# An attention and FFN kernel: the first 16 score tiles transposed by TensorE, the weights' low halves made by GpSimd, the weight conversions later in the order

## The chip, the cores and the metric

The kernel runs on one core of a Trainium2 chip. The metric is the device time of one execution in microseconds (us), taken as the median of several runs. The engines of the core are TensorE (PE in the profile, with its weight loads as PEld), VectorE (DVE), ScalarE (ACT), GpSimd (POOL) and SyncE (SP), whose queue issues all DMAs here.

## The reference

Attention with a threshold, followed by a feed-forward network (FFN) over the same tokens:

```python
# q, k, v: (8 batches, 8 heads, 576 tokens, 64), float32
scores = scale * q @ k^T
thresh = max(scores, axis=-1) - tau
scores = where(scores >= thresh, scores, -1e9)
attn   = exp(scores - max) / (sum(exp(scores - max)) + 1e-9)
x      = (attn @ v) as (4608 tokens, 512)        # heads side by side
# w_in: (512, 2048), w_out: (2048, 512): they arrive as float64
h      = relu(x @ w_in)
out    = (s * h * h + b) @ w_out                 # (4608, 512) float32
```

## The kernel before, in words

**Order.** Every piece of work is handed to a planner (`Plan`) with an engine, a cost in ns, the keys that it reads and writes, and a due number `at`. The planner runs the pieces through its own model: whenever an engine is free, it takes from those that are ready the one with the lowest due number. The result is a fixed order for each engine; on the chip each engine goes through its list in that order. Due numbers count tiles: tile i is the i-th score tile.

**Attention.** A visit is one batch, one pair of heads and one half (256) of the first 512 queries. It has four tiles, each 128 queries of one head by all 576 keys; half of the visits have a fifth tile for the last 64 queries of both heads. There are 64 visits and 288 tiles. For a tile:

- PE makes the scores (L211; the fifth tile L202), into PSUM banks `s0` and `s1`.
- DVE scales them, takes the row minimum of the negated scores and copies to `sm` (L221).
- ACT adds tau to that minimum (L225, one column) and takes the exponential into `em` (L227).
- DVE masks and sums (L230), then takes the reciprocal (L233).
- POOL multiplies the rows by it (L234), in place in `em`. `sm` and `em` have two buffers each.
- DVE transposes `em` in 32 x 32 blocks into `tr` (L238 and, for the last 64 keys, L240).
- Four DMAs on SP's queue (L244) bring the blocks of `tr` to their partitions in `er`.

When a visit's tiles are in `er`, PE multiplies with V (PV, L255) into bank `pv`, and ACT copies the result to `x` (L259, tails L262).

**Loads.** A visit's loads (L180 to L192: K, Q, two of V and, for the last 64 keys of V, two more) are due six tiles ahead. K's columns are permuted on the host, before the launch.

**Weights.** The FFN is cut into 16 chunks of 128 hidden units. Chunk f has a load of w_in and one of w_out (L280, L283, 512 KB each, due at 2 + f). It is then converted from float64 to a high and a low half in the fp32r type, twice each step (for w_in and w_out): ACT L315, DVE L318, DVE L320, ACT L324 (the high half), DVE L326 (the low half: value minus high half). This conversion is due at `WEIGHTS_AT + WEIGHTS_EACH * f`, that is 6 + 1.2f.

**FFN.** A block is 256 tokens. Its x is split into a high and a low half (ACT L368, DVE L370: `stage`). Each of 16 steps multiplies x by one chunk of w_in (L385, bank `h`), ACT applies relu, square and the high half (L388, L390, L391), POOL makes the low half gl (L392), and PE multiplies by the chunk of w_out (L398, bank `o`). There are 18 blocks, 288 steps. Block 0 follows visit 3: its stage is due at 17.5, step f at 17.5 + 1.2f, and so it needs one new chunk at each step. Block 1 follows visit 7. During block 0, four sums over w_out's columns are also made on PE (L337).

**Filling.** Before and between the first tiles, PE runs matmuls without use (L468, `keep_busy`): 16 at the start and 5 after each of the first five tiles.

Of the kernel before, what the change touches and what calls it, by code (L numbers as in the profile page):

```python
# [14 lines left out]
LOAD_AHEAD = 6  # L15
SCORES_AHEAD, VALUES_AFTER = 1, 2
FFN_AFTER = 2.5
BUSY, BUSY_TILES, BUSY_EACH = 16, 5, 5
WEIGHTS_AT, WEIGHTS_EACH = 6, 1.2
FIRST_WEIGHTS = 4  # L20


# [77 lines left out]
def tile_attention_ffn(ctx: ExitStack, tc: tile.TileContext, qT, kT, v, tau, w_in, w_out, s, b, out):  # L100
    nc = tc.nc
    P = 128
# [23 lines left out]
    def const(name, shape, dt=F32):  # L126
        return cp.tile(shape, dt, name=name)
# [41 lines left out]
    class Visit:
        def __init__(self, n, bi, pair, u, tail):  # L170
            self.n, self.bi, self.pair, self.u, self.tail, self.end = n % 2, bi, pair, u, tail, False
            self.h2 = slice(2 * pair, 2 * pair + 2)
            self.kq = [("k", self.n), ("q", self.n)]
            self.kd = [("qd", self.n, j) for j in range(2)]
            self.kv = [("v", self.n, x) for x in range(4)]
            self.nb = (NB + (T if tail else 0)) // 32

        def load(self, at):
            n, bi, h2 = self.n, self.bi, self.h2
            dma(295, lambda: nc.sync.dma_start(out=kb[n], in_=kT[bi, h2].rearrange("h d s -> (h d) s")), [], [("k", n)], at)  # L180
            dma(131, lambda: nc.sync.dma_start(out=qb[n], in_=qT[bi, h2, :, self.u * NB:(self.u + 1) * NB].rearrange(
                "h d s -> (h d) s")), [], [("q", n)], at)
            if self.tail:
                for j in range(2):
                    dma(16, lambda j=j: nc.sync.dma_start(out=qd[n][j * D:(j + 1) * D, j * T:(j + 1) * T],
                                                          in_=qT[bi, 2 * self.pair + j, :, M:S]), [], [self.kd[j]], at)
            for j in range(2):
                dma(131, lambda j=j: nc.sync.dma_start(
                    out=vb[n][:, j, 0:NQ], in_=v[bi, 2 * self.pair + j, 0:M, :].rearrange("(c p) d -> p c d", p=P)),
                    [], [self.kv[j]], at + 1)  # L190
            for m in range(2):
                dma(16, lambda m=m: nc.sync.dma_start(  # L192
                    out=vb[n][:, :, NQ].rearrange("(k m) h d -> k m h d", m=4)[:, m],
                    in_=v[bi, h2, M + 32 * m:M + 32 * m + 32, :].rearrange("h k d -> k h d")), [], [self.kv[2 + m]], at + 1)
# [20 lines left out]
    def tile_of(vs, i, j, t):  # L215
        ps, ks_, st8 = bank[f"s{j}"], f"st{i % 6}", st[i % 6]
        sm_k, em_k, tr_k = f"sm{i % 2}", f"em{i % 2}", f"tr{i % 2}"
        sb_, eb, to = sm[i % 2], em[i % 2], tr[i % 2]
        ev = eb[:, 0:S]

        dve((745, 830), lambda: nc.vector.tensor_scalar(  # L221
            out=sb_[:, 0:S].rearrange("p (a b) -> p a b", a=2), in0=ps[:, :, 0:HS],
            scalar1=nsc, scalar2=None, op0=ALU.mult, op1=ALU.min, accum_out=st8[:, 0:1]),
            [f"s{j}", "nsc"], [sm_k, (ks_, 0)], i - 0.6)
        act((287, 370), lambda: nc.scalar.activation(out=st8[:, 1:2], in_=st8[:, 0:1], func=AF.Identity, bias=tau0),  # L225
            [(ks_, 0), "nsc"], [(ks_, 1)], i - 0.4)
# [3 lines left out]
        dve2((940, 1010), lambda: nc.vector.scalar_tensor_tensor(  # L230
            out=eb, in0=sb_, scalar=st8[:, 1:2], in1=eb, op0=ALU.is_le, op1=ALU.mult,
            accum_out=st8[:, 2:3]), [sm_k, em_k, (ks_, 1)], [em_k, (ks_, 2)], i)
        dve((110, 165), lambda: nc.vector.reciprocal(out=st8[:, 4:5], in_=st8[:, 2:3]), [(ks_, 2)], [(ks_, 4)], i)  # L233
        pool((900, 940), lambda: nc.gpsimd.tensor_scalar(  # L234
            out=ev, in0=ev, scalar1=st8[:, 4:5], scalar2=zero, op0=ALU.mult, op1=ALU.add), [em_k, (ks_, 4)], [em_k], i)

        def blocks():
            nc.vector.transpose(out=to[:, :, 0:NQ].rearrange("p m c q -> p m (c q)"),  # L238
                                in_=ev[:, 0:M].rearrange("p (m r) -> p m r", m=4))
            nc.vector.transpose(out=to[:, 0:2, NQ], in_=ev[:, M:S].rearrange("p (m q) -> p m q", m=2))  # L240
        dve((915, 980), blocks, [em_k], [tr_k], i + 0.5)
        for n in range(4):
            jj, e = (n // 2, NB // 32 + n % 2) if t is None else (j, 4 * t + n)
            plan.add("SP", (450, 2600), lambda n=n, jj=jj, e=e: nc.sync.dma_start(  # L244
                out=er[:, vs.n, jj, e], in_=to[32 * n:32 * n + 32].rearrange("p m c q -> p m (c q)")),
                [tr_k], [("er", vs.n, jj, e)], i + 0.5)

    def with_v(vs, at):
        n, nb = vs.n, vs.nb
        ps = bank["pv"]  # L250

        def products():
            for c in range(5):
                for j in range(2):
                    nc.tensor.matmul(ps[j * D:(j + 1) * D, 0:32 * nb], vb[n][:, j, c], er[:, n, j, 0:nb, 32 * c:32 * c + 32],  # L255
                                     start=(c == 0), stop=(c == 4))
        pe(10.5 * 0.85 * 32 * nb, products, vs.kv + [("er", n, j, e) for j in range(2) for e in range(nb)], ["pv"], at)
        xk = xs[vs.bi, vs.u]
        act((340, 420), lambda: nc.scalar.copy(out=xb[xk][:, vs.pair], in_=ps[:, 0:NB]), ["pv"], [("x", xk, vs.pair)], at)  # L259
        if vs.tail:  # L260
            q = vs.bi % 4
            act((220, 300), lambda: nc.scalar.copy(out=xt[:, vs.pair, q * T:(q + 1) * T], in_=ps[:, NB:NB + T]), ["pv"],  # L262
                [("xt", q, vs.pair)], at)
# [22 lines left out]
    def weights(f, at):  # L286
# [11 lines left out]
        def tmp():  # L298
            if ("tmp", f) not in lazy:
                lazy["tmp", f] = sb(tag, [P, 2, DM], F32)  # L300
            return lazy["tmp", f]
# [10 lines left out]
            return tmp().bitcast(I32)[:, u]  # L312
        for u, k in (0, "i"), (1, "o"):
            kr, kt = (f"w{f}", k), (tag, u)
            act((570, 670), lambda u=u: nc.scalar.activation(  # L315
                out=tmp()[:, u], in_=words(1, u).bitcast(F32), func=AF.Prelu, scale=2.0 ** -112, alpha=-2.0 ** 32),
                [kr], [kt] if u else [tag, kt, (tag, 1)], at)
            dve2((410, 480), lambda u=u: nc.vector.tensor_scalar(  # L318
                out=y(u), in0=y(u), scalar1=3, scalar2=None, op0=ALU.logical_shift_left), [kt], [kt], at)
            dve2((610, 690), lambda u=u: nc.vector.scalar_tensor_tensor(  # L320
                out=y(u), in0=words(0, u), scalar=29, in1=y(u), op0=ALU.logical_shift_right, op1=ALU.bitwise_or),
                [kr, kt], [kt], at)
        for u, k in (0, "i"), (1, "o"):
            act((520, 620), lambda u=u: nc.scalar.copy(out=w()[:, u, 0], in_=tmp()[:, u]), [(tag, u)],  # L324
                wkeys(f) if not u else [(f"w{f}", "o")], at)
            dve2((620, 700), lambda u=u: nc.vector.tensor_tensor(out=w()[:, u, 1], in0=tmp()[:, u],  # L326
                                                                 in1=w()[:, u, 0].bitcast(F32), op=ALU.subtract),
                 [(tag, u), (f"w{f}", k)], [(f"w{f}", k)], at)


# [235 lines left out]
```

## Time and profile before

| what | value |
|---|---|
| median of 3 runs | 1329.89 us (1328.1 to 1330.42) |
| the profiled execution, its time | 1331.58 us |
| its span in the trace | 1329.8 us |
| PE busy | 1250.4 us (94%) |
| VectorE, ScalarE, GpSimd busy | 832.7, 680.9, 503.0 us |
| mean granted TensorE clock | 0.968 |

How to read the lines: in the slices, each digit is the busy share of a fortieth of the span in tenths. In the windows, a row has the stretch and its length, the busy time (and number of instructions) of PE, PEld, DVE, ACT and POOL, the granted TensorE clock, the mean busy share of the 16 DMA engines and the GB/s that they moved. A timeline row has the start in us, the duration in us, the engine, the line, the operation, what it writes and reads, shapes and the count; a count over 1 means several merged into one row; in brackets the idle time before it and what ended it. Durations of neighbours on one engine can overlap a little, since an instruction begins before the one ahead of it has drained. A group row of the page has line, engine, operation, output and input, shapes and count, then the busy time in us and the mean ns of one, then idle time before. A row by line or tile has the count, the shortest, median and longest duration in ns, and the first and last start in us.

### The profile page before, as it was taken

How to read it: one execution, taken by the hardware profiler on the slowest of the kernel's cores; microseconds unless marked ns; L12 is line 12 of the kernel's file. 1: busy time of each engine (PE TensorE's matmuls, PEld its weight loads, DVE VectorE, ACT ScalarE, POOL GpSimd, SP SyncE). 2: the span in 40 equal slices, each digit the busy share in tenths (PEclk: the TensorE clock that was granted, in tenths of full speed). 3: DMA queues.
4: the chain of work that ended last, by engine and by line, in shares of the span. 5: the costliest groups of instructions: out<-in, count | busy, mean ns of one | idle time of the engine just before them, and what ended most of it. 6: DMA issues, size and time to landing. Idle time of an engine off the chain costs nothing.

```text
span 1329.8 us, 24065 instructions
## 1 busy us (share of the span) xinstructions
PE 1250.4 (94%) x7689; PEld 970.6 (73%) x7689; DVE 832.7 (63%) x2205; ACT 680.9 (51%) x1639; POOL 503.0 (38%) x577
## 2 busy tenths in 40 slices
PE   6448999999999999999999999999999999999997
PEld 4226766777777777777778777787777777777886
DVE  7998675767666675756666565756666575763011
ACT  4655554555445554555455544545555455554343
POOL 2212333434344444443434344434444344443210
PEclk7559999999999999999999999999999999999999
DMA  7885455555455455544454544544455444542000
GB/s 207 265 271 149 121 132 127 130 134 129 130 137 148 126 128 139 140 122 112 134 131 120 126 122 112 153 117 121 123 140 127 118 117 120 137 119 61 17 17 16
DMA packets 283822, 169.41 MB, mean 127 GB/s; under 512 B 105008, under 2 KB 268848, under 8 KB 283696
## 3 DMA queue, kind: packets, MB, share of 16 engines
q1 hardware_dynamic: 283696, 167.88, 47.9%
q8 instruction: 61, 1.00, 0.3%
q14 instruction: 65, 0.53, 0.1%
HBM read 63.96 MB, written 9.44 MB: 55 GB/s over the span
## 4 chain that ended last, share of the span: by engine, by line
PE 78%; DVE 7%; DMA 6%; SPq 4%; issue 2%; ACT 2%; POOL 0%; DVEq 0%; ACTq 0%; POOLq 0%
PE o L398 28%; PE h L385 27%; PE pv L255 12%; PE s L211 9%; DMA er<-tr 5%; SPq L244 3%; PE s L202 2%; DVE sm L221 1%; DVE em L230 1%; DVE tr L238 1%; ACT em L227 1%; DMA w<-in_moe_w_in_dram 1%; DVE w L326 1%; DMA out_dram<-oo 1%; SPq L192 0%
## 5 line engine op out<-in xcount | busy, mean ns | idle before, releaser
L385 PE MATMUL h<-xh,w 128*128 128x256 f32 x2304 | 475.3, 289 | 11.0 <-ACT g L388 10.0
L234 POOL TENSOR_SCALAR em<-em,st,zero 128x576 f32<-128x576 f32 x288 | 283.6, 986 | 459.0 <-DVE st L233 308.6
L385 PEld LDWEIGHTS h<-xh,w 128*128 128x128 f32 x2304 | 377.6, 191 | 55.8 <-ACT g L390 20.0
L398 PE MATMUL o<-w,gh 128*128 128x512 f32 x1152 | 371.1, 403 | 4.4 <-DVE oo L409 4.0
L392 POOL TENSOR_TENSOR gl<-g,gh 128x256 fp32r<-128x256 f32 x272 | 220.6, 812 | 313.1 <-issue 141.8
L227 ACT ACTIVATE em<-sm,st 128x576 f32<-128x576 f32 x288 | 222.7, 773 | 203.6 <-DVE sm L221 128.6
L385 PE MATMUL h<-xl,w 128*128 128x256 f32 x1152 | 326.1, 283 | 0.3 <-DVE xl L370 0.3
L221 DVE TENSOR_SCALAR_CACHE_REDUCE sm<-s,nsc 128x576 f32<-128x576 f32 x288 | 227.5, 809 | 123.2 <-PE s L211 83.2
L238 DVE STREAM_TRANSPOSE tr<-em 128x512 f32<-128x512 f32 x288 | 204.1, 709 | 156.6 <-DMA er<-tr 93.6
L230 DVE SCALAR_TENSOR_TENSOR em<-sm,st,em 128x577 f32<-128x577 f32 x288 | 248.0, 862 | 85.9 <-ACT st L225 53.9
L398 PEld LDWEIGHTS o<-w,gh 128*128 128x128 f32 x1152 | 199.5, 189 | 68.8 <-issue 21.0
L388 ACT ACTIVATE g<-h 128x256 f32<-128x256 f32 x288 | 109.7, 381 | 269.6 <-PE h L385 264.2
L398 PE MATMUL o<-w,gl 128*128 128x512 f32 x576 | 225.3, 391 | 1.3 <-POOL gl L392 1.3
L385 PEld LDWEIGHTS h<-xl,w 128*128 128x128 f32 x1152 | 219.9, 191 | 8.5 <-DVE xl L370 0.5
L211 PE MATMUL s<-k,q 64*128 64x288 f32 x1024 | 175.5, 446 | 33.3 <-DVE sm L221 24.3
L255 PE MATMUL pv<-er,v 128*64 128x256 f32 (+1 forms) x1280 | 188.0, 424 | 14.7 <-DMA er<-tr 12.4
L255 PEld LDWEIGHTS pv<-er,v 128*64 128x64 f32 x1280 | 99.0, 141 | 93.4 <-issue 41.2
L211 PEld LDWEIGHTS s<-k,q 64*128 64x128 f32 x1024 | 96.3, 193 | 81.2 <-DVE sm L221 32.2
L398 PEld LDWEIGHTS o<-w,gl 128*128 128x128 f32 x576 | 108.2, 188 | 28.4 <-POOL gl L392 3.1
L391 ACT CAST gh<-g 128x256 fp32r<-128x256 f32 x288 | 115.9, 402 | 15.1 <-PE o L398 8.9
L390 ACT ACTIVATE g<-g 128x256 f32<-128x256 f32 x288 | 119.2, 414 | 6.6
L225 ACT ACTIVATE st<-st,tau 128x1 f32<-128x1 f32 x288 | 81.5, 286 | 41.1 <-DVE sm L221 41.0
(46 smaller groups left out, 452.1 us busy)
## 6 DMA issues: line engine op xcount, KB each, us to landing
er<-tr SPq DMA_DIRECT2D x1152, 80.0 KB, 2.2
k<-in_k_dram SPq DMA_DIRECT2D x64, 288.0 KB, 3.1
v<-in_v_dram SPq DMA_DIRECT2D x128, 128.0 KB, 2.5
q<-in_q_dram SPq DMA_DIRECT2D x64, 128.0 KB, 2.4
w<-in_moe_w_in_dram SPq DMA_DIRECT2D x16, 512.0 KB, 4.9
w<-in_moe_w_out_dram SPq DMA_DIRECT2D x16, 512.0 KB, 4.7
out_dram<-oo SPq DMA_DIRECT2D x32, 256.0 KB, 2.3
v<-in_v_dram SPq DMA_DIRECT2D x128, 16.0 KB, 2.2
```

Of the source, the lines that this page charges most:

```text
L211: nc.tensor.matmul(bank[f"s{j}"][:, hf, 0:HS], qb[n][r, t * P:(t + 1) * P], kb[n][r, cs], start=True, stop=True)
L221: dve((745, 830), lambda: nc.vector.tensor_scalar(out=sb_[:, 0:S].rearrange("p (a b) -> p a b", a=2), in0=ps[:, :, 0:HS], scalar1=nsc, sca ...
L227: act((780, 870), lambda: nc.scalar.activation(out=ev, in_=sb_[:, 0:S], func=AF.Exp, bias=st8[:, 0:1], scale=-1.0), [sm_k, (ks_, 0)], [em_ ...
L230: dve2((940, 1010), lambda: nc.vector.scalar_tensor_tensor(out=eb, in0=sb_, scalar=st8[:, 1:2], in1=eb, op0=ALU.is_le, op1=ALU.mult, accum ...
L234: pool((900, 940), lambda: nc.gpsimd.tensor_scalar(out=ev, in0=ev, scalar1=st8[:, 4:5], scalar2=zero, op0=ALU.mult, op1=ALU.add), [em_k, ( ...
L238: nc.vector.transpose(out=to[:, :, 0:NQ].rearrange("p m c q -> p m (c q)"), in_=ev[:, 0:M].rearrange("p (m r) -> p m r", m=4))
L255: nc.tensor.matmul(ps[j * D:(j + 1) * D, 0:32 * nb], vb[n][:, j, c], er[:, n, j, 0:nb, 32 * c:32 * c + 32], start=(c == 0), stop=(c == 4))
L385: nc.tensor.matmul(ps, w[:, c, :], x[:, c, :], start=(i == 0), stop=(i == 3 * NC - 1))
L390: act((290, 390), lambda: nc.scalar.activation(out=g, in_=g, func=AF.Square), [f"g{k}"], [f"g{k}"], at)
L391: act((310, 405), lambda: nc.scalar.copy(out=hi, in_=g), [f"g{k}"], [f"gh{k}"], at)
L392: do((715, 750), lambda: eng.tensor_tensor(out=lo, in0=g, in1=hi.bitcast(F32), op=ALU.subtract), [f"g{k}", f"gh{k}"], [f"gl{k}"], at)
L398: nc.tensor.matmul(bank["o"][:, t, :], a[:, ts_], w, start=(f == 0 and i == 0), stop=(f == NF - 1 and i == 2))
```

## The change

Four things, all of which concern the opening of the kernel:

1. For the 16 tiles of the first four visits (`PE_VISITS = 4`), DVE's transposes and the four DMAs per tile go. PE transposes `em` instead, 128 columns at a time and the last 64 keys apart (five transposes a tile, into the halves of bank `o` and into bank `h`), with an identity that lies in the unused third x buffer. ACT copies the results to `er` (two copies a tile). V is loaded in another order of rows for these visits, with one DMA for the last 64 keys instead of two. The threshold addition of these tiles goes from ACT to DVE.
2. The low halves of all weight chunks are made by GpSimd instead of VectorE (L326 before).
3. `WEIGHTS_AT` goes from 6 to 12, and the planner's costs for the conversion's pieces go up.
4. 24 filling matmuls at the start, and none between the tiles; two memsets of V's last rows on GpSimd before visits 4 and 5.

```diff
-BUSY, BUSY_TILES, BUSY_EACH = 16, 5, 5
-WEIGHTS_AT, WEIGHTS_EACH = 6, 1.2
+BUSY, BUSY_TILES, BUSY_EACH = 24, 0, 5
+PE_VISITS = 4
+WEIGHTS_AT, WEIGHTS_EACH = 12, 1.2
...
+    ident = xb[2][:, 0, 0:P]
...
+            self.pe = n < PE_VISITS
...
+                rows = "(p c) d -> p c d" if self.pe else "(c p) d -> p c d"
+                dma(131, lambda j=j, rows=rows: nc.sync.dma_start(
+                    out=vb[n][:, j, 0:NQ], in_=v[bi, 2 * self.pair + j, 0:M, :].rearrange(rows, p=P)),
                     [], [self.kv[j]], at + 1)
+            if self.pe:
+                dma(32, lambda: nc.sync.dma_start(out=vb[n][0:T, :, NQ], in_=v[bi, h2, M:S, :].rearrange("h k d -> k h d")),
+                    [], self.kv[2:], at + 1)
+                return
...
+        if vs.pe:
+            dve((140, 210), lambda: nc.vector.tensor_scalar(
+                out=st8[:, 1:2], in0=st8[:, 0:1], scalar1=tau0, scalar2=None, op0=ALU.add), [(ks_, 0), "nsc"], [(ks_, 1)], i - 0.4)
+        else:
+            act((287, 370), lambda: nc.scalar.activation(out=st8[:, 1:2], in_=st8[:, 0:1], func=AF.Identity, bias=tau0),
+                [(ks_, 0), "nsc"], [(ks_, 1)], i - 0.4)
...
+        if vs.pe:
+            tp, tt = bank["o"][:, i % 2].rearrange("p (c q) -> p c q", c=NQ), bank["h"][0:T, 0:P]
+
+            def transposes():
+                nc.tensor.transpose(out=tt, in_=ev[:, M:S], identity=ident)
+                for c in range(NQ):
+                    nc.tensor.transpose(out=tp[:, c], in_=ev[:, c * P:(c + 1) * P], identity=ident)
+            pe(600, transposes, [em_k, "ident"], ["h", ("o", i % 2)], i + 0.5)
+            e = er[:, vs.n, j, 4 * t:4 * t + 4].rearrange("p n (c q) -> p c n q", c=5)
+            ke = [("er", vs.n, j, 4 * t + n) for n in range(4)]
+            act((220, 300), lambda: nc.scalar.copy(out=e[0:T, NQ], in_=tt.rearrange("p (n q) -> p n q", n=4)), ["h"], ke, i + 0.5)
+            act((640, 730), lambda: nc.scalar.copy(out=e[:, 0:NQ], in_=tp.rearrange("p c (n q) -> p c n q", n=4)),
+                [("o", i % 2)] + ke, ke, i + 0.5)
+            return
...
-            act((570, 670), lambda u=u: nc.scalar.activation(
+            act((665, 750), lambda u=u: nc.scalar.activation(
...
-            dve2((410, 480), lambda u=u: nc.vector.tensor_scalar(
+            dve2((480, 550), lambda u=u: nc.vector.tensor_scalar(
...
-            dve2((610, 690), lambda u=u: nc.vector.scalar_tensor_tensor(
+            dve2((700, 780), lambda u=u: nc.vector.scalar_tensor_tensor(
...
-            act((520, 620), lambda u=u: nc.scalar.copy(out=w()[:, u, 0], in_=tmp()[:, u]), [(tag, u)],
+            act((615, 700), lambda u=u: nc.scalar.copy(out=w()[:, u, 0], in_=tmp()[:, u]), [(tag, u)],
...
-            dve2((620, 700), lambda u=u: nc.vector.tensor_tensor(out=w()[:, u, 1], in0=tmp()[:, u],
-                                                                 in1=w()[:, u, 0].bitcast(F32), op=ALU.subtract),
+            pool((1400, 1440), lambda u=u: nc.gpsimd.tensor_tensor(out=w()[:, u, 1], in0=tmp()[:, u],
+                                                                   in1=w()[:, u, 0].bitcast(F32), op=ALU.subtract),
...
+    pool((500, 600), lambda: make_identity(nc, ident), [], ["ident"], -9.5)
...
+    for n in range(2):
+        events.append((visits[PE_VISITS - 1].last + 0.15, lambda n=n: pool(
+            (200, 240), lambda: nc.gpsimd.memset(vb[n][:, :, NQ], 0.0), [], [("v", n, 2), ("v", n, 3)],
+            visits[PE_VISITS + n].first - 5)))
```

More of the change, by code (lines that the diff above doesn't have):

```diff
@@ L7 @@
 from concourse._compat import with_exitstack
+from concourse.masks import make_identity
 F32 = mybir.dt.float32
@@ L187, in load @@
             for j in range(2):
-                dma(131, lambda j=j: nc.sync.dma_start(
-                    out=vb[n][:, j, 0:NQ], in_=v[bi, 2 * self.pair + j, 0:M, :].rearrange("(c p) d -> p c d", p=P)),
+                rows = "(p c) d -> p c d" if self.pe else "(c p) d -> p c d"
+                dma(131, lambda j=j, rows=rows: nc.sync.dma_start(
+                    out=vb[n][:, j, 0:NQ], in_=v[bi, 2 * self.pair + j, 0:M, :].rearrange(rows, p=P)),
                     [], [self.kv[j]], at + 1)
+            if self.pe:
+                dma(32, lambda: nc.sync.dma_start(out=vb[n][0:T, :, NQ], in_=v[bi, h2, M:S, :].rearrange("h k d -> k h d")),
+                    [], self.kv[2:], at + 1)
+                return
             for m in range(2):
@@ L224, in tile_of @@
             [f"s{j}", "nsc"], [sm_k, (ks_, 0)], i - 0.6)
-        act((287, 370), lambda: nc.scalar.activation(out=st8[:, 1:2], in_=st8[:, 0:1], func=AF.Identity, bias=tau0),
-            [(ks_, 0), "nsc"], [(ks_, 1)], i - 0.4)
+        if vs.pe:
[4 more added lines that the diff above has]
+                [(ks_, 0), "nsc"], [(ks_, 1)], i - 0.4)
         act((780, 870), lambda: nc.scalar.activation(
@@ L253, in products @@
             for c in range(5):
+                r = slice(0, T if vs.pe and c == NQ else P)
                 for j in range(2):
-                    nc.tensor.matmul(ps[j * D:(j + 1) * D, 0:32 * nb], vb[n][:, j, c], er[:, n, j, 0:nb, 32 * c:32 * c + 32],
+                    nc.tensor.matmul(ps[j * D:(j + 1) * D, 0:32 * nb], vb[n][r, j, c], er[r, n, j, 0:nb, 32 * c:32 * c + 32],
                                      start=(c == 0), stop=(c == 4))
@@ L258, in with_v @@
         xk = xs[vs.bi, vs.u]
-        act((340, 420), lambda: nc.scalar.copy(out=xb[xk][:, vs.pair], in_=ps[:, 0:NB]), ["pv"], [("x", xk, vs.pair)], at)
+        act((340, 420), lambda: nc.scalar.copy(out=xb[xk][:, vs.pair], in_=ps[:, 0:NB]), ["pv"],
+            [("x", xk, vs.pair)] + (["ident"] if xk == 2 else []), at)
         if vs.tail:
```

## The prediction

> **What bounds the kernel now.** I read the page's slices first: where is TensorE (PE) not full?
>
> ```profile
> span 1329.8 us, 24065 instructions
> PE   6448999999999999999999999999999999999997
> DVE  7998675767666675756666565756666575763011
> ```
>
> Besides the last, only the first four slices of 33 us are open. The windows split them at the first FFN matmul, which the timeline puts at 105.89 us; the second block's first one is at 191.56 us.
>
> ```profile
> 8.00:106.00 98.00, 51.57 (x180) 27.72 (x180) 93.88 (x226) 55.20 (x104) 20.80 (x20) 0.60 0.84 255
> 106.00:190.00 84.00, 80.18 (x472) 60.42 (x472) 58.86 (x151) 44.47 (x106) 30.23 (x35) 1.00 0.49 126
> 190.00:1330.00 1140.00, 1112.36 (x7004) 877.17 (x7004) 679.52 (x1828) 579.97 (x1431) 450.39 (x505) 1.00 0.45 116
> 105.89 0.38 PE L385 MATMUL h<-xh,w 128*128 128x256 f32 x1 [0.99 <-ACT xh L368]
> 191.56 0.38 PE L385 MATMUL h<-xh,w 128*128 128x256 f32 x1
> ```
>
> Columns: busy PE, PEld, DVE, ACT, POOL; then granted clock, DMA share, GB/s. From 8 to 106 VectorE (DVE) is busy 93.88 of 98 us (96%): it is the bound, with PE at a clock of 0.60 waiting. From 106 on PE is the bound (95%, then 98%). So the change, all of which ends with the first block, is worth what it does to the time 191.56, when block 1 starts; from there on the same work follows on a full PE. Block 0 itself lasts 191.56 - 105.89 = 85.7 us.
>
> The chain of waits from 0 to 106 says what stands between DVE's pieces:
>
> ```profile
> by line: DMA er<-tr 12.0%; DMA w<-in_moe_w_in_dram 10.8%; DVE w L326 8.2%; issue 8.0%; DVE tr L238 7.6%; DVE em L230 7.4%; DVE sm L221 6.9%; SPq L244 6.8%; DVE xh L320 3.5%; PE pv L255 3.4%; DMA tau_t<-in_tau_dram 3.2%; DVE xh L318 3.1%; AC
> ```
>
> The steps to be removed (er by DMA, tr, w L326) are on it. But DVE fills the same time, so a DMA taken from the chain only hands it to DVE; what counts is DVE's work and what can delay it.
>
> **A resource that no row names: DVE and GpSimd (POOL) exclude each other.**
>
> ```profile
> 25.13 1.29 DVE L326 TENSOR_TENSOR w<-xh,w 128x512 fp32r<-128x512 f32 x2
> 26.34 1.30 DVE L230 SCALAR_TENSOR_TENSOR em<-sm,st,em 128x577 f32<-128x577 f32 x1
> 25.36 1.68 POOL L234 TENSOR_SCALAR em<-em,st,zero 128x576 f32<-128x576 f32 x1 [2.58 <-DVE st L233]
> 96.74 0.82 DVE L230 SCALAR_TENSOR_TENSOR em<-sm,st,em 128x577 f32<-128x577 f32 x1
> 110.17 0.99 DVE L318 TENSOR_SCALAR xh<-xh 128x512 int32<-128x512 int32 x1
> 110.15 0.73 POOL L392 TENSOR_TENSOR gl<-g,gh 128x256 fp32r<-128x256 f32 x1 [0.44 <-ACT gh L391]
> 100.16 0.42 DVE L318 TENSOR_SCALAR xl<-xl 128x512 int32<-128x512 int32 x1
> L234 POOL TENSOR_SCALAR em<-em,st,zero x19: 825/826/1683, 11.0 to 98.4; 128x576 f32<-128x576 f32 x19
> L392 POOL TENSOR_TENSOR gl<-g,gh x272: 723/739/1245, 110.2 to 1274.8; 128x256 fp32r<-128x256 f32 x136
> L320 DVE SCALAR_TENSOR_TENSOR xh<-w,xh x16: 673/688/895, 19.0 to 111.4; 128x512 int32<-128x512 int32 x16
> L326 DVE TENSOR_TENSOR w<-xh,w x16: 644/684/1015, 25.1 to 113.6; 128x512 fp32r<-128x512 f32 x16
> ```
>
> POOL's 0.825 us operation, issued at 25.36, sat through the two L326 and ended at 27.04; the L230 begun at 26.34 was then held too (1.30 for 0.82). At 110.17 an L318 of 0.42 took 0.99 beside a POOL operation that ran at full speed. So I treat POOL and DVE's L230, L318, L320, L326 and L370 as one resource, "the port"; L221 (from PSUM) and the transposes are not in it. The Trainium skill has this as a rule that speaks against the change (SBUF — State Buffer, "SBUF: two separate sides": the shared pair is "an exclusive lock, not a bandwidth split"). The trace agrees, with the 1.68 and 0.99 us just shown.
>
> **The change part by part**, as work up to block 1's start (36 tiles, 16 weight chunks, 16 FFN steps).
>
> 1. *Low halves to POOL.* Removed from DVE: 32 x 0.684 = 21.9 us. Added on POOL: 32 subtractions of 512 columns, a shape that the trace lacks. Bounds: above 0.825 (a one-input operation of 576 columns), up to 2 x 0.739 = 1.48. I take 1.40, near the two-input row: 44.8 us. (The Trainium skill, GPSIMD Engine Reference, "Elementwise — side-by-side cycle accounting", gives 2.6 cycles an element at 1.2 GHz, an estimate of 1.1 us; the sum below would be 10 us less.) Behind each on POOL's queue wait the tiles' normalizations (L234) and the steps' gl (L392).
>
> 2. *DVE transposes of 16 tiles out, a threshold addition in.*
>
> ```profile
> 24.32 0.70 DVE L238 STREAM_TRANSPOSE tr<-em 128x512 f32<-128x512 f32 x1
> 24.94 0.20 DVE L240 STREAM_TRANSPOSE tr<-em 128x64 f32<-128x64 f32 x1
> 25.07 0.11 DVE L233 RECIPROCAL st<-st 128x1 f32<-128x1 f32 x1
> L225 ACT ACTIVATE st<-st,tau 128x1 f32<-128x1 f32 x288 | 81.5, 286 | 41.1 <-DVE sm L221 41.0
> L340 ACT COPY bias_t<-h 128x512 f32<-128x512 f32 x1 | 0.6, 587 | 0.1
> L262 ACT COPY xt<-pv 128x64 f32<-128x64 f32 x32 | 7.0, 218 | 0.0
> 96.44 2.51 SPq L244 DMA_DIRECT2D er<-tr  x4
> er<-tr SPq DMA_DIRECT2D x1152, 80.0 KB, 2.2
> 99.02 2.29 PE L211 MATMUL s<-k,q 64*128 64x288 f32 x8 [8.81 <-DVE sm L221]
> 101.24 3.65 PE L255 MATMUL pv<-er,v 128*64 128x256 f32 x20
> L385 PEld LDWEIGHTS h<-xh,w 128*128 128x128 f32 x2304 | 377.6, 191 | 55.8 <-ACT g L390 20.0
> ```
>
> DVE: -16 x 0.90 + 16 x 0.11 (a one-column operation, as the reciprocal) = -12.6 us. With part 1 its busy time from 8 to 190 falls from 93.88 + 58.86 = 152.7 to 118 us. ScalarE (ACT): 16 x (0.587 + 0.218 - 0.286) = +8.3 on 55.2 + 44.5 = 99.7, so 108 us: no bound. SP: 16 x 2.51 = 40 us of issuing and 64 x 80 KB = 5.2 MB less; the DMA share of 0.84 beside it only falls. The weight loads keep their places, and the queue gets to them sooner.
> PE: 5 transposes a tile, no row. Low end 5 x 0.191 = 0.96 us (a pass like a weight load); high end, by L211 at the low clock: 8 passes of 288 columns, two at a time, in 2.29 us, so 0.57 a pass, 0.25 for 128 columns, and ten such 2.5 us. I take 1.4. With 2.29/2 of scores and 3.65/4 of PV a tile then costs PE 3.5 us, and 16 end at 8 + 56 = 64 us: just hidden behind the port (68, below); at the high end not. (The Trainium skill, TensorE: Matmul & The Clock Gate, "Terms", has transpose mode 4x faster for fp32: 2.5 would be 0.6.)
>
> 3. *Conversions later* (due 12 + 1.2f instead of 6 + 1.2f; block 0's stage is due at 17.5). Conversions 0 to 4 instead of 0 to 9 come ahead of the stage. It removes nothing: it lets FFN start earlier and pushes eleven conversions into block 0, which PE bounded until now. The higher planner costs move order only; I give them nothing, bounded by the range.
>
> 4. *Small.* Identity (POOL, from the 0.2 us memsets an estimate of 0.5 to 2 us, hidden ahead of 8 us); two memsets before visits 4 and 5 (0.2 us each, behind PV 2 and 3 on POOL: some 2 us of its queue at worst); fewer dummy matmuls (PE is idle there; the lower clock is in the 3.5); V's four loads of visits 0 to 3 in longer runs, one DMA less per visit. Zero, behind the port.
>
> ```profile
> L448 POOL MEMSET v<- 128x128 f32 x2 | 0.4, 205 | 0.0
> 190.25 0.69 DVE L370 TENSOR_TENSOR xl<-x,xh 128x512 fp32r<-128x512 f32 x1
> ```
>
> **The sum.** Port work. A tile: 0.825 + 0.82 = 1.645. A conversion: on DVE 2 x (0.42 + 0.688) = 2.22, before + 2 x 0.69 = 3.60, after + 2 x 1.40 = 5.02. Before: 36 x 1.645 + 16 x 3.60 + 16 x 0.739 + 4 x 0.69 = 131; after 154. DVE's rows overlap by some 0.09 (two L326 take 1.29), over 136 and 104 operations: 119 and 145 us. So the change takes 35 us from DVE and gives 26 to the port, which becomes the bound of the opening: from 8 us on, 145 us at least, 153. How full can it run? From 8 to 106 it held 20 tiles and 14 conversions, 83 - 9 = 74 us of 98 (0.76), with DVE as the bound; with DVE at 118 of some 165 us it can be fuller, short of 1. I take 0.88: 8 + 145/0.88 = 173. FFN starts when 18 tiles and 5 conversions are through: 54.7 - 3 = 52, 8 + 52/0.88 = 67, say 68; block 0 then takes 105 us instead of 85.7. Block 1 starts 191.6 - 173 = 18.6 us earlier.
>
> The profiled execution took 1331.58 us (span 1329.8), 1.7 over the median of 1329.89. 1331.6 - 18.6 - 1.7 = 1311.
>
> **The rivals.**
> - *PE sets block 0's pace after all* (POOL's operations fall beside L221 and the transposes, or are cheap). FFN starts by DVE alone: 18 tiles of 1.89 (0.82 + 0.81 + 0.15 + 0.11) and 5 x 2.22 are 45, and some 7 of the tiles' chain, 60; block 1 at 60 + 85.7 = 146: 46 us gained, 1284. For: in the trace the normalization mostly runs beside L221. Against: the port's sum of 153.
> - *The transposes hold PE.* At 2.5 us a tile PE needs 4.6, FFN starts at 84, and the port's remaining 93/0.88 = 106 us follow: block 1 at 190, no gain; partly so, 1318 to 1331. Speaks for it: clock 0.60 with PE half idle.
> - *No gain:* the port runs at 0.79, little over the 0.76 that it had: 8 + 145/0.79 = 191.5, the time of now, 1330. For: nobody orders POOL's and DVE's turns. Against: DVE, which held it at 0.76, has slack now.
> - *Slower:* POOL's subtraction is dearer. Place: 22 of them in block 0's first eleven steps, each holding DVE and, through gl, PE. At 0.88, block 1 is later than 191.6 + 2.7 once the port passes 164 us: 101 + 32p = 164, p = 1.97 us; at 2.3 us block 1 is at 206, 1345. For: L392's maximum, doubled, is 2.5. Against: its median doubled, 1.48.
>
> **How the numbers follow.** 0.2% (2.7 us) is what a measurement here can tell from no change. Forecast, 1297 to 1322: 0.55. PE-paced: 0.20. Transposes: 0.12, a third of it within 0.2%. No gain by the port: 0.06. Slower: 0.07. Faster 0.83, same 0.10, slower 0.07. The range, 1282 to 1328, takes in PE-paced and most of the transposes' case; outside stay some 0.06 below and 0.13 above.
>
> **What would show it.** In the profile after: the first FFN matmul near 68 us; block 1's first near 173; low halves of 1.4 us on POOL with longer ones among them; L318 and L320 with means well over 0.42 and 0.69 while POOL is at work; PE with idle time in block 0 that ends on POOL or DVE; from 190 on as before. Wrong if FFN starts after 80 us, if block 0 keeps to 86 us, or if the later stretches' PE share differs by more than 3 us.

## The result, and the profile after

The changed kernel takes 1315.99 us (median of 4 runs, 1314.95 to 1318.1) against 1329.83 for the one before: a ratio of 0.9897, 95% interval 0.9879 to 0.9915. That is 13.8 us faster; 18.6 were forecast (1311). The profiled execution took 1318.1 us, span 1316.1.

The head and the slices of the page after:

```profile
span 1316.1 us, 24095 instructions
...
PE   7689799999999999999999999999999999999997
...
DVE  6888876666676766657575656766666576663011
...
POOL 3676534344444444434344343534445344443210
```

PE's opening is now ragged rather than open: FFN work starts in the third slice instead of the fourth. The timeline gives the first FFN matmul and the first one of block 1, the windows what lies between:

```profile
67.23 0.83 PE L415 MATMUL h<-xh,w 128*128 128x256 f32 x1
175.67 0.39 PE L415 MATMUL h<-xh,w 128*128 128x256 f32 x1
8.00:67.00 59.00, 43.24 (x239) 25.71 (x240) 51.36 (x132) 41.92 (x85) 33.95 (x31) 0.89 0.83 276
67.00:176.00 109.00, 91.19 (x492) 66.93 (x492) 93.69 (x199) 62.96 (x142) 67.03 (x59) 0.92 0.48 129
176.00:1316.00 1140.00, 1113.37 (x6996) 875.02 (x6994) 678.32 (x1824) 578.28 (x1427) 448.05 (x505) 1.00 0.45 116
```

FFN starts 38.7 us earlier (67.2 instead of 105.9), but block 0 now lasts 108.4 us instead of 85.7. Block 1 starts 15.9 us earlier (175.7 instead of 191.6). Of these, 2.2 are lost again later: from block 1 to the end of the span it is 1140.4 us, before 1138.2. So all of the gain arises ahead of block 1, and 23 of the 39 us that FFN won go back in block 0.

Two things have changed in block 0: ten of the sixteen conversions now fall into it (by L350, six begin ahead of FFN; before, fourteen did), and pieces on VectorE and GpSimd have become longer. The second is in the groups (0 to 180 us):

```profile
L356 POOL TENSOR_TENSOR w<-xh,w 128x512 fp32r<-128x512 f32 x16 | 23.3, 1472 | 3.3 <-ACT w L354 3.2
L356 POOL TENSOR_TENSOR w<-xl,w 128x512 fp32r<-128x512 f32 x16 | 22.7, 1429 | 7.8 <-ACT w L354 7.7
L350 DVE SCALAR_TENSOR_TENSOR xl<-w,xl 128x512 int32<-128x512 int32 x16 | 16.6, 1045 | 0.1
L350 DVE SCALAR_TENSOR_TENSOR xh<-w,xh 128x512 int32<-128x512 int32 x16 | 15.9, 1000 | 0.1
L348 DVE TENSOR_SCALAR xl<-xl 128x512 int32<-128x512 int32 x16 | 12.0, 758 | 2.7 <-ACT xl L345 2.7
L348 DVE TENSOR_SCALAR xh<-xh 128x512 int32<-128x512 int32 x16 | 10.3, 647 | 3.4 <-ACT xh L345 3.3
L256 PE MATMUL o<-x,em 128*128 128x128 f32 x64 | 11.5, 310 | 0.8 <-ACT er L261 0.8
L254 PE MATMUL h<-x,em 128*64 128x128 f32 x16 | 5.1, 320 | 10.8 <-POOL em L247 9.2 <-ACT er L260 1.5
```

L350 and L348 are the same instructions as L320 and L318 before, which took 0.68 and 0.42 us with nothing beside them. Now their means are 1.0 and 0.7. One pair in the timeline shows it happening:

```profile
132.27 3.03 POOL L356 TENSOR_TENSOR w<-xl,w 128x512 fp32r<-128x512 f32 x2 [2.33 <-ACT w L354]
132.50 1.66 DVE L350 SCALAR_TENSOR_TENSOR xh<-w,xh 128x512 int32<-128x512 int32 x1
134.09 1.50 DVE L348 TENSOR_SCALAR xh<-xh 128x512 int32<-128x512 int32 x1
135.29 1.56 POOL L247 TENSOR_SCALAR em<-em,st,zero 128x576 f32<-128x576 f32 x1
```

While two subtractions run on GpSimd (1.5 us each), L350 is held to 1.66 us and L348 to 1.50, one after the other; then the normalization waits in its turn (1.56 for 0.82). These waits are not the whole of block 0's 23 us: it lasts 112.9 us with the low halves on VectorE (low_on_dve, below) and 102.5 us with no subtraction at all (low_by_act).

### The profile page after: what moved, and what is told of

Same layout as the page of the kernel before. It is cut to its first block, busy times and chain, and to the rows that moved or that the text cites. A ratio compares the mean times of both kernels' runs of the same rounds, so it can differ in the third digit from the quotient of the medians.

```text
span 1316.1 us, 24095 instructions
## 1 busy us (share of the span) xinstructions
PE 1254.2 (95%) x7752; PEld 972.6 (74%) x7752; DVE 824.5 (63%) x2157; ACT 684.6 (52%) x1655; POOL 551.0 (42%) x613
## 3 DMA queue, kind: packets, MB, share of 16 engines
q8 instruction: 62, 1.02, 0.3%
## 4 chain that ended last, share of the span: by engine, by line
PE 77%; DVE 7%; DMA 4%; SPq 4%; issue 3%; ACT 3%; POOL 1%; DVEq 0%; POOLq 0%; ACTq 0%
PE o L428 27%; PE h L415 27%; PE pv L284 12%; PE s L220 9%; SPq L272 3%; DMA er<-tr 3%; PE s L211 2%; DVE em L243 1%; DVE sm L230 1%; ACT em L240 1%; DMA out_dram<-oo 1%; DVE tr L266 1%; DVE xl L350 1%; DVE oo L439 1%; SPq L201 1%
## 5 line engine op out<-in xcount | busy, mean ns | idle before, releaser
L415 PE MATMUL h<-xh,w 128*128 128x256 f32 x2304 | 478.3, 290 | 18.7 <-ACT g L418 12.2
L243 DVE SCALAR_TENSOR_TENSOR em<-sm,st,em 128x577 f32<-128x577 f32 x288 | 250.3, 870 | 89.0 <-ACT st L238 54.1
L230 DVE TENSOR_SCALAR_CACHE_REDUCE sm<-s,nsc 128x576 f32<-128x576 f32 x288 | 227.2, 808 | 121.6 <-PE s L220 83.4
L266 DVE STREAM_TRANSPOSE tr<-em 128x512 f32<-128x512 f32 x272 | 192.7, 709 | 144.9 <-DMA er<-tr 78.7
L284 PE MATMUL pv<-er,v 128*64 128x256 f32 (+1 forms) x1280 | 185.2, 416 | 8.6 <-DMA er<-tr 5.4
L220 PE MATMUL s<-k,q 64*128 64x288 f32 x1024 | 167.0, 437 | 6.5 <-DVE sm L230 6.5
L284 PEld LDWEIGHTS pv<-er,v 128*64 128x64 f32 x1280 | 95.0, 138 | 87.1 <-issue 26.3
L220 PEld LDWEIGHTS s<-k,q 64*128 64x128 f32 x1024 | 93.3, 190 | 47.9 <-DVE sm L230 10.9
L238 ACT ACTIVATE st<-st,tau 128x1 f32<-128x1 f32 x272 | 76.7, 286 | 26.3 <-DVE sm L230 26.0
```

Source lines behind the costliest of these rows:

```text
L220: nc.tensor.matmul(bank[f"s{j}"][:, hf, 0:HS], qb[n][r, t * P:(t + 1) * P], kb[n][r, cs], start=True, stop=True)
L230: dve((745, 830), lambda: nc.vector.tensor_scalar(out=sb_[:, 0:S].rearrange("p (a b) -> p a b", a=2), in0=ps[:, :, 0:HS], scalar1=nsc, sca ...
L243: dve2((940, 1010), lambda: nc.vector.scalar_tensor_tensor(out=eb, in0=sb_, scalar=st8[:, 1:2], in1=eb, op0=ALU.is_le, op1=ALU.mult, accum ...
L284: nc.tensor.matmul(ps[j * D:(j + 1) * D, 0:32 * nb], vb[n][r, j, c], er[r, n, j, 0:nb, 32 * c:32 * c + 32], start=(c == 0), stop=(c == 4))
L415: nc.tensor.matmul(ps, w[:, c, :], x[:, c, :], start=(i == 0), stop=(i == 3 * NC - 1))
```

## The experiments

All times below are medians; "block 1" is the first FFN matmul of block 1 in the profiled execution. Each job also ran the kernel before, and the ratio refers to that. For comparison: before, block 1 at 191.6; the change, 0.9897 and 175.7.

| kernel | time, us | ratio, 95% interval | block 1, us |
|---|---|---|---|
| low_on_dve | 1316.68 | 0.9885 [0.9870, 0.9899] | 174.8 |
| at_6 | 1316.24 | 0.9881 [0.9867, 0.9896] | 178.8 |
| pool_low_alone | 1333.43 | 1.0019 [1.0004, 1.0033] | 196.6 |
| pe_transposes_alone | 1316.66 | 0.9894 [0.9876, 0.9912] | 174.9 |
| low_by_act | 1303.82 | 0.9805 [0.9781, 0.9829] | 165.8 |
| pool_twice | 1342.64 | 1.0102 [1.0082, 1.0123] | 204.0 |
| split_low | 1315.23 | 0.9902 [0.9878, 0.9926] | 179.8 |
| er_two_queues | 1315.04 | 0.9892 [0.9871, 0.9914] | 177.4 |
| dead_transposes | 1327.99 | 0.9975 [0.9962, 0.9988] | 186.8 |
| pool_memsets | 1323.85 | 0.9941 [0.9928, 0.9953] | 185.1 |
| norm_on_act | 1323.51 | 0.9939 [0.9924, 0.9955] | 184.7 |
| norm_on_act_split | 1321.42 | 0.9926 [0.9914, 0.9938] | 176.2 |

The two profiled executions of split_low and er_two_queues were 4 us over their medians, so their block 1 is some us late. Two expectations below have block 1 at 176.7 for low_on_dve and at 176.9 for pe_transposes_alone; the traces have 174.8 and 174.9, which changes no verdict.

### Which part of the change does it?

**low_on_dve**: the changed kernel, low halves back on VectorE.

```diff
-            pool((1400, 1440), lambda u=u: nc.gpsimd.tensor_tensor(out=w()[:, u, 1], in0=tmp()[:, u],
+            dve2((700, 780), lambda u=u: nc.vector.tensor_tensor(out=w()[:, u, 1], in0=tmp()[:, u],
```

> The changed kernel, with the low halves of the weights given back to VectorE; all else as changed. Theory PORT (VectorE and GpSimd exclude each other, and that sum bounds the opening): the port's work up to block 1 falls from 145 to 119 us while VectorE's rises from 118 to 140, so VectorE bounds again at about 0.96: block 1 at 8 + 140/0.96 = 154 to 160 us instead of 175.7, and the time is about 1297 (1290 to 1304), faster than the changed kernel. Rival LOAD (what counts is how much work VectorE has; GpSimd runs beside it): 22 us come back onto the busiest engine, block 1 at 185 to 195, 1325 to 1336, slower than the changed kernel.

Measured 1316.68: neither range. Giving the work back costs nothing and gains nothing. The windows from 8 to 176 us of the changed kernel and of low_on_dve, and low_on_dve's conversion groups in that stretch:

```profile
8.00:176.00 168.00, 134.43 (x730) 92.64 (x731) 145.05 (x330) 104.89 (x227) 100.98 (x89) 0.91 0.60 180
```

```profile
8.00:176.00 168.00, 132.16 (x734) 92.02 (x735) 146.18 (x365) 105.83 (x228) 53.12 (x57) 0.91 0.60 179
```

```profile
L356 DVE TENSOR_TENSOR w<-xh,w 128x512 fp32r<-128x512 f32 x16 | 12.2, 784 | 1.1 <-ACT w L354 1.0
L356 DVE TENSOR_TENSOR w<-xl,w 128x512 fp32r<-128x512 f32 x16 | 11.8, 754 | 1.0 <-ACT w L354 0.9
L350 DVE SCALAR_TENSOR_TENSOR xl<-w,xl 128x512 int32<-128x512 int32 x16 | 11.5, 723 | 0.0
L350 DVE SCALAR_TENSOR_TENSOR xh<-w,xh 128x512 int32<-128x512 int32 x16 | 11.0, 696 | 0.0
L348 DVE TENSOR_SCALAR xl<-xl 128x512 int32<-128x512 int32 x16 | 7.4, 476 | 0.1
L348 DVE TENSOR_SCALAR xh<-xh 128x512 int32<-128x512 int32 x16 | 7.0, 461 | 0.4 <-ACT xh L345 0.4
```

VectorE is busy for 146.2 us with the subtractions and for 145.1 without. It lost 12.2 + 11.8 = 24.0 us of work, and its L350 and L348 grew from 36.9 to 54.8 us: 17.9 came back as waiting, and part of the rest in the mask (L243, mean 0.89 to 0.93) and in L400 (2.6 to 4.0 us for four). That refutes LOAD (22 us of work would have to be worth 9 to 20 us). It also refutes what PORT expected here: VectorE did not run at 0.96, but at 146.2 / 168 = 0.87. From 100 to 110 us it was idle half of the time:

```profile
100.00:110.00 10.00, 3.68 (x19) 1.91 (x15) 5.09 (x13) 3.97 (x9) 1.78 (x2) 0.77 0.47 119
```

**at_6**: `WEIGHTS_AT` back to 6.

```diff
-WEIGHTS_AT, WEIGHTS_EACH = 12, 1.2
+WEIGHTS_AT, WEIGHTS_EACH = 6, 1.2
```

> The changed kernel with the conversions due at 6 + 1.2f again. PORT: the sum up to block 1 is the same 145 us, only its order differs: FFN starts later (near 90 us instead of 67), block 1 within 5 us of 175.7, the time 1311 to 1321. Rival ORDER (the gain came from letting FFN start early): block 1 near 90 + 86 = 176 is the same by this too only if block 0 then runs at PE's pace; if the first part is slower than 90, the time is 1322 to 1332.

Measured 1316.24, as PORT expects. FFN starts at 81.6 (near 90 was expected), block 1 at 178.8. Starting FFN 14 us sooner with the later due numbers is worth nothing measurable, because the conversions put off then fall into block 0: it takes 97.1 us here, 108.4 in the change.

**pool_low_alone**: the kernel before, with only the low halves moved.

```diff
-            dve2((620, 700), lambda u=u: nc.vector.tensor_tensor(out=w()[:, u, 1], in0=tmp()[:, u],
+            pool((1400, 1440), lambda u=u: nc.gpsimd.tensor_tensor(out=w()[:, u, 1], in0=tmp()[:, u],
```

> The kernel before with one part of the change: the low halves on GpSimd. Transposes, due numbers and costs as before. PORT: 21 tiles and 14.5 conversions ahead of FFN are 99 us of port work instead of 77, at 0.88 FFN starts near 120 instead of 106, block 0 is PE-bound: block 1 at 200 to 207, the time 1337 to 1348, slower than before. Rival LOAD: VectorE has 20 us less ahead of FFN, which starts near 86: about 1310.

Measured 1333.43, 0.2% slower (0.04 to 0.33%). LOAD (1310) is refuted; PORT has the direction, but several times the size: FFN starts at 109.3, not 120. VectorE is busy 86.0 us from 8 to 106 instead of 93.9, and nothing comes of it. The size was missed because the port was fuller than 0.88: ahead of FFN the trace has 20 masks (L230), 22 normalizations, 28 subtractions and 57 pieces of L318 and L320. At the prediction's prices and overlap, with 1.27 us for a subtraction, that is an estimate of 95 us of port work in 101 us.

**pe_transposes_alone**: transposes by PE, low halves on VectorE, due numbers at 6.

```diff
-WEIGHTS_AT, WEIGHTS_EACH = 12, 1.2
+WEIGHTS_AT, WEIGHTS_EACH = 6, 1.2
...
-            pool((1400, 1440), lambda u=u: nc.gpsimd.tensor_tensor(out=w()[:, u, 1], in0=tmp()[:, u],
+            dve2((700, 780), lambda u=u: nc.vector.tensor_tensor(out=w()[:, u, 1], in0=tmp()[:, u],
```

> The change without two of its parts: low halves on VectorE, conversions due at 6 + 1.2f; transposes by TensorE stay. PORT: VectorE bounds the stretch ahead of FFN: 18 tiles and 10 conversions are 70 us, at 0.96 FFN starts at 81 to 86 us, block 0 takes 86 to 90: block 1 at 167 to 176, the time 1306 to 1316: as good as the whole change or better. Rival LOAD: the low halves on GpSimd carried much of the gain, so without them the time is 1318 or more.

Measured 1316.66, just above PORT's range and below LOAD's 1318, so this run does not decide between them. But one of the three parts, with the small items and the planner costs that stay in, carries the whole gain.

### What in the transposes is worth it?

**dead_transposes**: as pe_transposes_alone, with VectorE's transposes put back as work that nobody reads.

```diff
             pe(600, transposes, [em_k, "ident"], ["h", ("o", i % 2)], i + 0.5)
+            def dead():
+                nc.vector.transpose(out=to[:, :, 0:NQ].rearrange("p m c q -> p m (c q)"),
+                                    in_=ev[:, 0:M].rearrange("p (m r) -> p m r", m=4))
+                nc.vector.transpose(out=to[:, 0:2, NQ], in_=ev[:, M:S].rearrange("p (m q) -> p m q", m=2))
+            dve((915, 980), dead, [em_k], [tr_k], i + 0.5)
```

> pe_transposes_alone, with VectorE's transposes of the first 16 tiles put back as dead work: they write tr, and nobody reads it; TensorE's transposes still feed er, and the 64 er transfers stay out. Theory VECTOR (the gain is the 14.4 us that VectorE lost): at 0.96 they cost 15 us, block 1 at 188 to 194 instead of 176.9, the time 1328 to 1334, the whole gain is gone. Rival TRANSFER (the gain is the 64 er transfers and their waits, 12% of the chain of before): 1314 to 1320.

Measured 1327.99, just short of VECTOR's range: 11.3 of the 14.8 us go again, with the 64 er transfers still out. Its groups from 8 to 100 us show the work put back:

```profile
L259 DVE STREAM_TRANSPOSE tr<-em 128x512 f32<-128x512 f32 x16 | 11.2, 702 | 1.8 <-POOL em L247 1.8
L261 DVE STREAM_TRANSPOSE tr<-em 128x64 f32<-128x64 f32 x16 | 3.2, 200 | 0.0
```

14.4 us of VectorE cost 11.3 (10.8 by the two ratios, give or take 3). The remaining 3.4 us (0.9975 against 1) are what the transfers, the filling matmuls, the planner costs and all the rest can be worth together.

### Does GpSimd's subtraction really hold VectorE, and at what price?

**low_by_act**: the low half written as a plain copy by ScalarE; it leaves out the 32 subtractions.

```diff
-            pool((1400, 1440), lambda u=u: nc.gpsimd.tensor_tensor(out=w()[:, u, 1], in0=tmp()[:, u],
-                                                                   in1=w()[:, u, 0].bitcast(F32), op=ALU.subtract),
-                 [(tag, u), (f"w{f}", k)], [(f"w{f}", k)], at)
+            act((615, 700), lambda u=u: nc.scalar.copy(out=w()[:, u, 1], in_=tmp()[:, u]),
+                [(tag, u), (f"w{f}", k)], [(f"w{f}", k)], at)
```

> The changed kernel, with each low half written by ScalarE as a plain copy: it leaves out the 32 subtractions, and so takes their load off both VectorE and GpSimd (ScalarE gets 32 x 0.615 = 20 us). Theory BALANCE (VectorE's own work plus its waits for the port set block 1; wherever the subtraction is put, it costs VectorE about 25 us): VectorE keeps 118 us and few waits, block 1 at 148 to 157 instead of 176, the time 1290 to 1299. Rival FIXED (block 1's start is set outside the low halves: TensorE's path through visits 4 to 7, or the queue of the er transfers): block 1 at 172 to 178, the time 1313 to 1319.

Measured 1303.82. The subtraction is worth 12 us, after what ScalarE's 32 copies cost, so FIXED is refuted; but block 1 is at 165.8, not 148 to 157, and BALANCE misses as well. Without the subtractions VectorE has this left:

```profile
8.00:165.00 157.00, 130.80 (x718) 89.19 (x719) 122.63 (x328) 117.45 (x256) 49.84 (x57) 0.93 0.63 191
```

It is busy 122.6 of 157 us (0.78), TensorE 130.8, ScalarE 117.5. No engine is full. I take it that from here on the handing over between engines counts, tile by tile; no run tests that.

**pool_twice**: each subtraction done twice on GpSimd.

```diff
+            for _ in range(2):
-            pool((1400, 1440), ...
+                pool((1400, 1440), ...
```

> The changed kernel, with each low half made twice by GpSimd (the same subtraction again): 32 x 1.3 = 42 us more on GpSimd, nothing more elsewhere. BALANCE, with the port: 145 + 42 = 187 us of port work, at 0.88 block 1 at 215 to 222, the time 1353 to 1363. If GpSimd merely ran beside VectorE: GpSimd's own sum is some 140 us up to block 1, short of 168, and the time stays 1314 to 1322.

Measured 1342.64, slower than the kernel before, and between the two ranges. That GpSimd merely runs beside VectorE is refuted; of some 41 us added (32 x 1.27), 27 appear (28 at block 1), where BALANCE had expected 37 or more. A doubled subtraction also makes its chunk ready later, which this run does not separate. L350 and L348 grow further, to means of 1.0 to 1.26 us; its groups from 8 to 200 us:

```profile
L350 DVE SCALAR_TENSOR_TENSOR xl<-w,xl 128x512 int32<-128x512 int32 x16 | 20.1, 1255 | 0.1
L348 DVE TENSOR_SCALAR xh<-xh 128x512 int32<-128x512 int32 x16 | 18.2, 1150 | 3.6 <-ACT xh L345 3.6
L350 DVE SCALAR_TENSOR_TENSOR xh<-w,xh 128x512 int32<-128x512 int32 x16 | 17.0, 1070 | 0.1
L348 DVE TENSOR_SCALAR xl<-xl 128x512 int32<-128x512 int32 x16 | 16.1, 1013 | 4.5 <-ACT xl L345 4.3
```

**pool_memsets**: the same extra time on GpSimd, by memsets, which read nothing.

```diff
...
+            def sets():
+                nc.gpsimd.memset(xb[2][:, 2:4], 0.0)
+                nc.gpsimd.memset(xb[2][:, 2:4], 0.0)
+                nc.gpsimd.memset(xb[2][:, 2], 0.0)
+            pool((1400, 1440), sets, [], ["scratch"], at)
```

> The changed kernel with 32 x 1.4 us more on GpSimd, as in pool_twice, but of memsets, which read nothing: after each subtraction 1,280 columns of an unused x buffer are set to zero. If pool_twice lost its 26 us to GpSimd's own queue (normalizations and gl come later), or if any GpSimd instruction holds VectorE: 1338 to 1346. If it is reading that holds VectorE's two-input instructions: 1316 to 1326.

Measured 1323.85, in the range of reading: 8 us over the change and 19 under pool_twice (6 and 21 by the ratios), so GpSimd's own queue isn't what pool_twice lost most of its time to. That leaves the second subtraction's hold on VectorE, and whatever its later chunks cost. Its groups from 8 to 200 us:

```profile
L350 DVE SCALAR_TENSOR_TENSOR xl<-w,xl 128x512 int32<-128x512 int32 x16 | 16.3, 1021 | 0.1
L350 DVE SCALAR_TENSOR_TENSOR xh<-w,xh 128x512 int32<-128x512 int32 x16 | 16.1, 1005 | 0.2
L348 DVE TENSOR_SCALAR xl<-xl 128x512 int32<-128x512 int32 x16 | 15.8, 998 | 1.1 <-ACT xl L345 1.1
L348 DVE TENSOR_SCALAR xh<-xh 128x512 int32<-128x512 int32 x16 | 14.3, 898 | 2.0 <-ACT xh L345 1.9
...
L362 POOL MEMSET x<- 128x512 f32 x29 | 16.2, 559 | 1.7
L361 POOL MEMSET x<- 128x512 f32 x28 | 15.0, 534 | 0.6
L363 POOL MEMSET x<- 128x256 f32 x29 | 9.7, 334 | 1.7
```

The memsets (0.56 + 0.53 + 0.33 = 1.43 us a time) leave L350, with two inputs, where the change had it (1.02 and 1.01; 1.05 and 1.00 there), but lengthen L348, with one input, to 1.00 and 0.90 (0.76 and 0.65 there). The Trainium skill has this distinction (SBUF — State Buffer, "SBUF: two separate sides"): a VectorE instruction with two SBUF inputs contends only with a GpSimd one that reads SBUF, one in a 2-port mode with any. The trace agrees for the two-input one; that L348 runs in a 2-port mode is named by no row. One place in the timeline shows both beside memsets alone:

```profile
51.96 0.69 POOL L362 MEMSET x<- 128x512 f32 x1
52.10 0.82 DVE L348 TENSOR_SCALAR xl<-xl 128x512 int32<-128x512 int32 x1
52.70 0.47 POOL L363 MEMSET x<- 128x256 f32 x1
52.85 0.67 DVE L350 SCALAR_TENSOR_TENSOR xh<-w,xh 128x512 int32<-128x512 int32 x1
```

All nine L350 that overlap memsets and nothing else of GpSimd's took 0.67 to 0.69 us, as with GpSimd idle; the six such L348 took 0.42 to 0.82. L350's mean of 1.0 comes from the subtractions, normalizations and gl that are still there.

### Is a better version in sight?

**split_low**: w_in's low halves on VectorE, w_out's on GpSimd.

```diff
+            if u:
+                pool((1400, 1440), ...gpsimd...
+            else:
+                dve2((700, 780), ...vector...
```

> The changed kernel, with w_in's low halves on VectorE and w_out's on GpSimd. BALANCE: VectorE has 129 us of its own and half of the waits, 142 to 146 in all: block 1 at 172 to 178, the time 1312 to 1319. By the port's sum alone (132 us at 0.88) block 1 would be at 158 and the time 1299.

Measured 1315.23: BALANCE. By now three placements (all on GpSimd, half, none) lie within 1.5 us.

**er_two_queues**: low_on_dve, and two of four er transfers of visits 4 to 7 issued from ScalarE's queue.

```diff
...
-            plan.add("SP", (450, 2600), lambda ...: nc.sync.dma_start(
+            on_act = vs.early and n % 2
+            plan.add("ACT" if on_act else "SP", (600, 2750) if on_act else (450, 2600),
+                     lambda ..., q=nc.scalar if on_act else nc.sync: q.dma_start(
```

> The changed kernel with the low halves on VectorE (as in low_on_dve), and in visits 4 to 7 two of a tile's four er transfers are issued from ScalarE's queue instead of SyncE's (0.6 us of ScalarE each, 40 of them). Rival QUEUE (SyncE's issuing, 0.6 us each and in order, holds visits 4 to 7): block 1 8 us or more ahead of low_on_dve's 176.7, the time 1302 to 1309. BALANCE: 1313 to 1319.

I had this rival from low_on_dve's chain of waits between 98 and 108 us:

```profile
by line: SPq L272 56.2%; SPq L193 10.8%; issue 7.3%; DVE sm L230 7.2%; SPq L201 6.7%; SPq L184 5.5%; DVE xl L348 5.5%; SPq L189 5.0%; DVE st L246 0.7%
```

SP's issuing makes up 84% of the chain there, yet relieving SP's queue gives nothing: 1315.04. QUEUE is refuted at the size that it expected; a smaller gain could be hidden by the 40 issues, 27 us in all, that ScalarE's queue now has.

**norm_on_act** and **norm_on_act_split**: the first 16 tiles' normalization on ScalarE, in the changed kernel and in split_low.

```diff
...
+        if vs.pe:
+            act((780, 870), lambda: nc.scalar.mul(out=ev, in_=ev, mul=st8[:, 4:5]), [em_k, (ks_, 4)], [em_k], i)
+        else:
             pool((900, 940), lambda: nc.gpsimd.tensor_scalar(
```

> The changed kernel with the normalization of the first 16 tiles on ScalarE instead of GpSimd (16 x 0.78 us): the port loses 13 us. PORT, by the runs so far (41 us of GpSimd's subtractions fewer gave 12, 45 more took 27): 3 to 8 us faster than the change, 1308 to 1313. If the port no longer binds in the first part, 1314 to 1319.

> split_low (w_in's low halves on VectorE, w_out's on GpSimd) with the normalization of the first 16 tiles on ScalarE. Port 119 us, VectorE 129: PORT expects 1304 to 1311, the fastest full kernel; if block 0 is held elsewhere, 1313 to 1318.

Both miss both of their ranges, 1323.51 and 1321.42: slower than the change, with 13 us less for the port. norm_on_act's timeline of GpSimd shows one cause:

```profile
41.33 1.27 POOL L359 TENSOR_TENSOR w<-xl,w 128x512 fp32r<-128x512 f32 x1 [5.75 <-PE pv L287]
55.53 0.21 POOL L513 MEMSET v<- 128x128 f32 x1 [12.93 <-issue]
55.73 1.27 POOL L359 TENSOR_TENSOR w<-xh,w 128x512 fp32r<-128x512 f32 x1
```

GpSimd stands idle for 12.9 us ahead of the memset of V's last rows, which in the fixed order comes before the next subtractions and follows the PV product that ended at 55.4. With fewer pieces on GpSimd the planner had put it there. Only 6 subtractions are begun before 60 us; the change has 10. That this alone makes the 7 us wasn't tried; ScalarE's 16 x 0.78 us are another candidate. For norm_on_act_split the loss can't even be placed: its profiled execution, the fastest of six, has block 1 at 176.2, half a us behind that of the change, the slowest of four.

## Why the prediction was right, point by point

- *What bounds, and that all is decided at block 1's start:* right for where it is decided: 15.9 us arise ahead of it, 2.2 are lost in the 1140 us after it. What bounds the opening is taken up below.
- *The exclusion of VectorE and GpSimd (the port):* right, and the heart of it. L348 and L350 grew as foreseen, and the time follows the amount of subtraction on GpSimd: 12 us less without it, 27 more with twice of it. Block 0 fell from PE's pace, so the PE-paced rival (1284) is out: it needed 86 us, and block 0 took 108.4. That the port alone lengthened it is not shown, since it takes 112.9 us in low_on_dve and 102.5 in low_by_act. The rival "slower" was to begin at 1.97 us for a subtraction, with block 1 at 194.3 (191.6 + 2.7): block 1 is at 175.7 with 1.27 us (the shortest in the trace) and at 204.0 with 2 x 1.27; on the line between, 194.3 lies at 2.1.
- *FFN's start:* 68 forecast, 67.2 measured. *Block 1:* 173 forecast, 175.7 measured.
- *GpSimd's price and the number of tiles:* 1.40 taken, 1.27 free, 1.43 to 1.47 with its own waits; with 1.27 the port's sum is 141 us. But the sum took 36 tiles up to block 1, and the trace has 39 masks and 41 normalizations there, an estimate of 6 us more: 147 us, and 147 / 167.7 = 0.88, the filling taken. Two mis-sized terms pull in opposite directions; what they leave is most of the 2.7 us at block 1.
- *TensorE's transposes:* 1.4 us a tile taken, (11.5 + 5.1) / 16 = 1.04 measured; that rival is out.
- *What failed is how the 18.6 us were thought to come about.* The sum took the opening as one port that is 0.88 full, whatever stands on it, with slack on VectorE. By that, giving the low halves back to VectorE (port 119, VectorE 140 at 0.96) had to win some 19 us more; it won nothing. Nor does the filling hold: counted as above, up to block 1, it is 0.75 in low_on_dve, 0.78 in pool_low_alone and 0.95 in pool_twice. That it was 0.88 in the change is luck. The step "with DVE at 118 of some 165 us it can be fuller" leaves out that VectorE's time includes its waiting for the port: it is busy 145 of 168 us either way, with its own work or held. And in block 0 neither of the two is the bound alone. The chain of waits by line, from 67 to 176 us of the change and from 62 to 175 us of low_on_dve:

```profile
by line: PE h L415 15.0%; PE pv L284 11.7%; PE o L428 9.5%; DVE xl L350 7.4%; PE s L220 6.9%; issue 6.6%; PE s L211 4.0%; DVE sm L230 3.9%; PE h L367 3.6%; DVE tr L266 3.1%; DVE xl L348 2.8%; DVE xl L400 2.4%; DVE xh L348 2.3%; ACT w L354 2
by line: SPq L272 9.5%; PE h L415 9.2%; DMA q<-in_q_dram 8.0%; DVE em L243 7.8%; DVE w L356 7.6%; DVE sm L230 7.2%; issue 7.1%; PE pv L284 6.3%; DVE tr L266 6.3%; DMA er<-tr 5.8%; DVE xl L350 5.4%; PE o L428 2.8%; DVE xl L348 2.2%; PE s L22
```

  In the change, PE's rows shown make up 51% of the chain. In low_on_dve VectorE's make up over a third; the er transfers, with their issuing, and a load of q are nearly a quarter. Two different chains thus reach block 1 at the same time (175.7 and 174.8), which no sum of the port's work could tell. So two of the change's three parts, which the sum credits together, are worth nothing; VectorE's 16 tiles of transposes are worth 11 of the 14 us.
- *Open:* what fills the last 13 to 22% of VectorE's time ahead of block 1. Issuing part of the er transfers elsewhere did not shorten it; PE, ACT and DVE hand over to each other there, and no single wait stood out.

## What to carry to other kernels

Work taken from one engine counted here only where the engine that took it did not hold the first one (the transposes on TensorE, not the subtractions on GpSimd): compare the means of untouched instructions (here L348, 0.47 us with the subtractions on VectorE, 0.70 with them on GpSimd), and look at the busy time of the relieved engine, which includes its waiting. Test the parts of a change one at a time; here one part carried all of it, and the sum that predicted the whole could not tell. And when pieces are moved between fixed orders, look at what now stands at the head of the queue they left.

## What the runs showed of the hardware that I had not expected

- Memsets on GpSimd lengthen VectorE's one-input instruction (means from 0.65 to 0.90 and from 0.76 to 1.00 us), not its two-input one (1.00 and 1.05 us without them, 1.01 and 1.02 with them; 0.67 to 0.69 beside memsets alone).
- GpSimd's two-input subtraction costs 0.73 us for 256 columns and 1.27 for 512: 2.1 ns a column and 0.2 us beside it.
- The granted clock from 8 to 67 us is 0.89 instead of 0.62, with fewer filling matmuls but 43.2 instead of 32.3 us of busy PE. It is 0.83 in pe_transposes_alone and 0.74 in dead_transposes, which is hardly faster than before; how much of it is the transposes' doing was not tried.
